# Attention in 32-wide tiles turned by VectorE, and Strassen's products in both expert layers with partial sums forked in PSUM

## The chip, the cores and the metric

The kernel runs on one core of a Trainium2 chip. Four engines compute: TensorE (PE; its weight loads are PEld), VectorE (DVE), ScalarE (ACT) and GpSimd (POOL). SyncE (SP) and POOL issue DMA transfers. Matrix products land in PSUM, eight banks of 128 partitions x 512 fp32 values; everything else lives in SBUF. The metric is the device time of one execution in microseconds.

## The reference

Inputs in fp32: q, k, v of shape (8 batches, 8 heads, 576 positions, 64), w_in (512 x 2048), w_out (2048 x 512).

```
scores = q @ k.T / 8;  kept only where 0 <= row - column < 64
attn   = softmax(scores) @ v                      # per batch and head
x      = attn, heads side by side                 # 4608 tokens x 512
h      = x @ w_in;  g = h * sigmoid(h)            # 4608 x 2048
out    = g @ w_out                                # 4608 x 512, fp32
```

## The kernel before

All products take bf16 operands. **Attention** goes by batch (8), by pairs of heads (4 a batch) and by groups of three blocks of 64 rows (3 a batch). A block of 64 query rows sees the 64 keys of its own block and of the block before, so its scores are a 128 x 64 product per head. `scores` (L359) does both heads of a pair in one matmul of 128 columns: k of the pair lies in `kt` with the two heads' 64 dimensions one above the other on the 128 partitions, and q lies in `qbd` as a block-diagonal, with zeros where the other head's dimensions are. `expo` (L377) takes the exponential on ACT, `masking` (L380) multiplies by the window's mask on DVE, `values` (L385) multiplies by v of both heads and a column of ones, `inverse` (L391) and the norm functions (L397, L414, L420) divide by the sum.

The dimensions of q and k must stand on partitions, tokens come in on partitions. Batches 0 and 1 of k and 0 to 3 of q are turned by TensorE (`turn_heads` L309, `turn_twos` L318) and copied out of PSUM (`lift_*`, L324 to L337); later ones are turned by DMA from SP (`turn_rows`, L270), q then spread by DVE (L278). The attention output is turned back by TensorE (`back`, `back_both`, L430, L441) or, from the end of batch 2 on, by DMA (`turn_o`, L435). The result, x with its 512 dimensions on partitions, is `bridge`.

**The expert layers** go by tiles of 512 tokens, nine of them. `first_layer` (L450) is plain: 16 x 4 matmuls of 512 columns a tile, `silu` (L456) after each four. `second_layer` (L459) is plain for tiles 0 to 4: 64 matmuls of 512 columns. Tiles 5 to 8 (`FAST`) use Strassen's seven products of half-size matrices in the Winograd form instead: `weight_sum` (L469) and `token_sum` (L476) make the sums of quarters on DVE, `product` (L484) makes seven times 16 matmuls of 256 columns, `keep_part` (L487) copies partial sums to SBUF and `join` (L494, L496) adds them on the way out.

**Order.** The class `Plan` places every operation on an engine's own list at build time, with costs and ranks written in the code; the chip then runs each engine's list in order, waiting on semaphores. Four PSUM banks (`at`) are for attention, four (`mp`) for the expert layers, until the attention is over. Until the first expert matmul, filler matmuls (L824) keep TensorE at work. POOL issues the loads of q, k, v and the weights, which change fp32 to bf16 on the way; SP issues two first loads, the turning DMAs and the stores.

Of the kernel before, what the change touches and what calls it, by code (L numbers as in the profile page):

```python
# [13 lines left out]

class Plan:

    def __init__(self, pools, rank, rank0, ahead):
        self.rank, self.rank0, self.pools = rank, {**rank0, **{c + "0": r for c, r in ahead.items()}}, pools
        self.queues = {}
        self.banks = [[] for _ in range(8)]
        self.count = 0
        self.now = 0.0

    def add(self, cls, us, fn, deps=(), lat=0.08, gate=None, dma=None, pool=None, table=None, b=0):
        if b > 1 and cls in ("cast", "lift", "spread", "mask", "norm"):
            lat = 0.2  # L30
        op = dict(us=us, first=self.rank[cls] + b if b or cls not in self.rank0 else self.rank0[cls], fn=fn, deps=[d for d in deps if d is not None], lat=lat, gate=gate, dma=dma,
                  pool=pool, table=table, seen=None, n=self.count, until=[], bank=None)
        self.count += 1
        self.queues.setdefault(cls, []).append(op)
        return op

    def add_filler(self, n, cls, us, fn, *args, **kw):

        for _ in range(n):
            op = self.add(cls, us, None, *args, **kw)  # L40
            op["until"], op["fn"] = [op], lambda e, op=op: fn(op)
        self.count -= n

    def done(self, ops):
        return all(d["seen"] is not None and d["seen"] <= self.now for d in ops)

    def run(self):
        head = {c: 0 for c in self.queues}
        engines = sorted({e for q in self.queues.values() for op in q for e in op["us"]})
        free = {e: 0.0 for e in engines}  # L50
        can = {e: [c for c, q in self.queues.items() if any(e in op["us"] for op in q)] for e in engines}
        table, left = "exp", self.count
        pipe = {True: 0.0, False: 0.0}
        events, order = [0.0], []
        while left:
            if not events:
                raise RuntimeError([(c, head[c], q[head[c]]["n"]) for c, q in self.queues.items() if head[c] < len(q)])
            now = self.now = heapq.heappop(events)
            while events and events[0] == now:
                heapq.heappop(events)  # L60
# [51 lines left out]
def kernel(ctx, tc, q, k, v, w_in, w_out, out):  # L112
    nc = tc.nc
# [768 lines left out]
```

## Time and profile before

| | us |
|---|---|
| median of 3 runs (lowest, highest) | 318.58 (318.53, 320.08) |
| span of the profiled execution | 315.5 |
| TensorE busy | 303.1 (96%) |
| VectorE busy | 200.5 (64%) |
| ScalarE busy | 188.4 (60%) |
| first expert matmul / last Strassen product's join, from the span's start | 23.23 / 310.61 |
| the one long gap on TensorE, in the slice from | 181 to 189 |

The profiled execution's own time is given as its span, from the first to the last instruction; the times of the runs are device times, which take in a little around it. Engine times in a group of instructions are the union of their intervals, and one instruction's duration holds its latency: matmuls are pipelined, so 16 of them in a row take far less than 16 durations. Where a price per matmul is wanted, the distance between rows of the chain or the timeline gives it.

### The profile page before, as it was taken

The numbers are of one execution on the slowest core, as the hardware profiler recorded it, in microseconds if no ns is written. First come the engines' busy times: TensorE is split into PE (matmuls) and PEld (weight loads), VectorE is DVE, ScalarE is ACT, GpSimd is POOL, SyncE is SP. The second block draws the span as 40 slices with busy tenths as digits, with TensorE's granted clock in tenths as the row PEclk, the third lists the DMA queues.
The fourth block names the chain that finished last, engine by engine and source line by source line (L and its number), as shares of the span: only waits on it lengthen the run. The fifth ranks groups of instructions, "written<-read, shape, count | busy, mean of one in ns | idle before, by whom it ended". The sixth has DMA issues, their size and how long they took to land.

```text
span 315.5 us, 6452 instructions
## 1 busy us (share of the span) xinstructions
PE 303.1 (96%) x2366; PEld 185.7 (59%) x2383; DVE 200.5 (64%) x573; ACT 188.4 (60%) x370; POOL 118.8 (38%) x159
## 2 busy tenths in 40 slices
PE   8999999999999999999999949999999999999993
PEld 4678656545565555645654535447964874684583
DVE  4684838946898899894894147956887323332422
ACT  8798786888757661767527732478346416515620
POOL 8957859676806797873465000000000000000000
PEclk9999999999999999999999988999999999999998
DMA  9999999999999999999999983310133012003003
GB/s 141 177 197 186 191 196 145 118 245 137 176 152 171 146 124 172 176 186 142 156 160 206 157 80 84 92 26 0 27 139 47 1 58 77 2 0 135 0 17 118
DMA packets 138112, 37.55 MB, mean 119 GB/s; under 512 B 122465, under 2 KB 133729, under 8 KB 138081
## 3 DMA queue, kind: packets, MB, share of 16 engines
q0 software_dynamic: 95712, 18.06, 78.1%
q1 hardware_dynamic: 42368, 19.08, 33.4%
q8 instruction: 19, 0.31, 0.4%
q14 instruction: 13, 0.10, 0.1%
HBM read 36.70 MB, written 9.44 MB: 146 GB/s over the span
## 4 chain that ended last, share of the span: by engine, by line
PE 87%; DVE 4%; DMA 4%; issue 1%; ACT 1%; POOL 0%; POOLq 0%; DVEq 0%
PE mp L450 30%; PE mp L459 20%; PE mp L484 10%; PE at L385 5%; PE at L484 5%; PE at L359 5%; PE at L450 4%; DMA vv<-in_v_dram 4%; DVE qbd L324 2%; PE at L824 1%; PE mp L824 1%; PE at L318 1%; DVE vv L345 1%; ACT qbd L324 1%; PE at L441 1%
## 5 line engine op out<-in xcount | busy, mean ns | idle before, releaser
L450 PE MATMUL mp<-bridge,w_in_sb 128*128 128x512 bf16 (+2 forms) x576 | 118.9, 355 | 0.6 <-ACT g L456 0.5
L450 PEld LDWEIGHTS <-w_in_sb 128*128 128x128 bf16 x640 | 60.1, 98 | 58.6 <-issue 1.3
L456 ACT ACTIVATE g<-mp 128x512 bf16<-128x512 f32 (+2 forms) x144 | 76.9, 552 | 26.4 <-PE mp L450 25.6
L459 PE MATMUL mp<-w_out_sb,g 128*128 128x512 bf16 x303 | 83.5, 382 | 0.6
L377 ACT ACTIVATE e<-at 128x384 bf16<-128x384 f32 x90 | 38.7, 498 | 14.1 <-PE at L359 13.5
L414 DVE TENSOR_TENSOR ox<-at,rc 64x192 bf16<-64x192 f32 x128 | 45.2, 353 | 2.4
L264 POOL DMA_DIRECT2D late<-in_k_dram x48 | 35.6, 746 | 22.6 <-DMA late<-in_k_dram 11.0
L282 POOL DMA_DIRECT2D vv<-in_v_dram x32 | 32.8, 1030 | 18.3 <-PE at L359 7.7
L459 PEld LDWEIGHTS <-g 128*128 128x128 bf16 x320 | 28.4, 98 | 17.2
L385 PEld LDWEIGHTS <-e 128*128 128x128 bf16 x288 | 22.6, 97 | 19.6 <-DVE e L380 6.7
L380 DVE TENSOR_TENSOR e<-e,mask 128x384 bf16<-128x384 bf16 x84 | 26.6, 348 | 11.8 <-ACT e L377 11.1
L385 PE MATMUL at<-vv,e 128*128 128x130 bf16 x273 | 29.8, 220 | 4.2 <-DVE e L380 4.0
L476 DVE TENSOR_TENSOR late<-g 128x512 bf16<-128x512 bf16 x32 | 13.5, 422 | 28.1 <-ACT g L456 28.0
L484 PEld LDWEIGHTS <-late 128*128 128x128 bf16 x256 | 24.8, 98 | 2.9
L264 POOL DMA_DIRECT2D late<-in_q_dram x32 | 23.8, 748 | 4.8 <-DMA vv<-in_v_dram 3.0
L359 PE MATMUL at<-qbd,kt 128*128 128x128 bf16 x252 | 24.4, 223 | 0.1
L391 DVE RECIPROCAL rc<-at 128x6 f32<-128x6 f32 x91 | 17.4, 194 | 10.6 <-PE at L385 7.5
L359 PEld LDWEIGHTS <-kt 128*128 128x128 bf16 x252 | 18.8, 100 | 8.8 <-issue 1.9
L499 ACT COPY ot<-mp 128x512 f32<-128x512 f32 x12 | 6.9, 586 | 25.9 <-PE mp L459 20.2
L484 PEld LDWEIGHTS <-g 128*128 128x128 bf16 x192 | 18.5, 98 | 2.6
L324 DVE COPY qbd<-at 64x288 bf16<-64x288 bf16 x26 | 12.5, 480 | 10.6 <-ACT qbd L324 7.1
L456 ACT ACTIVATE g<-at 128x512 bf16<-128x512 f32 x16 | 9.6, 597 | 11.6 <-PE at L450 11.6
(94 smaller groups left out, 318.8 us busy)
## 6 DMA issues: line engine op xcount, KB each, us to landing
out_dram<-ot SPq DMA_DIRECT2D x34, 256.0 KB, 2.6
vv<-in_v_dram POOLq DMA_DIRECT2D x32, 144.0 KB, 7.2
late<-in_k_dram POOLq DMA_DIRECT2D x48, 72.0 KB, 7.1
late<-in_q_dram POOLq DMA_DIRECT2D x32, 72.0 KB, 7.1
early<-in_q_dram POOLq DMA_DIRECT2D x15, 144.0 KB, 6.4
w_in_sb<-in_moe_w_in_dram POOLq DMA_DIRECT2D x8, 256.0 KB, 8.2
w_out_sb<-in_moe_w_out_dram POOLq DMA_DIRECT2D x8, 256.0 KB, 7.8
early<-in_k_dram POOLq DMA_DIRECT2D x7, 144.0 KB, 5.2
```

What stands on the lines that cost most here:

```text
L264: nc.gpsimd.dma_start(out=rows(i)[:, pj % 2, :, 64 * hh:64 * hh + 64], in_=(q, k)[kk][b, 2 * pj + hh].rearrange("(m p) d -> p m d", p=NR),)
L282: queue[e].dma_start(out=vv[b % NK][:, 2 * g0 + 1:2 * g1 + 1:2, 0:D], in_=v[b].rearrange("h s d -> (h s) d").rearrange("(g p) d -> p g d", ...
L324: copies[e](out=qbd[b % NK][64 * hh:64 * hh + 64, pj, hh].rearrange("x (p m) -> x p m", m=NM)[:, :, r::2], in_=at_bf16(op)[64 * r:64 * r + ...
L359: nc.tensor.matmul(at_sp(op)[:, x], lhsT=kt[b % NK][:, pj * S + t * 64:pj * S + t * 64 + 128], rhs=qbd[b % NK][:, pj, :, t * 64:t * 64 + 6 ...
L377: nc.scalar.activation(out=es[n % NE], in_=at_sp(op), func=ACTF.Exp, scale=scale)
L380: nc.vector.tensor_mul(es[n % NE], es[n % NE], mask0 if g == 0 else mask)
L385: nc.tensor.matmul(at_pv(op)[:, x], lhsT=es[n % NE][:, x].rearrange("p h i -> p (h i)"), rhs=vv[b % NK][:, s:s + NB + 1:NB, 0:D + 1], star ...
L414: nc.vector.tensor_mul(ox(n)[:, :, r], pv[r, :, hh, 0:D], rc[r, :, hh:hh + 1].to_broadcast([64, 3, 64]))
L450: nc.tensor.matmul(banks[bank["bank"]][:, lo:hi], lhsT=w_in_sb[:, c, ft * 128:(ft + 1) * 128], rhs=bridge[:, j * TB % NBR + lo // 64:j * T ...
L456: nc.scalar.activation(out=gts[gt][:, lo:hi], in_=banks[bank["bank"]][:, lo:hi], func=ACTF.Silu)
L459: nc.tensor.matmul(banks[bank["bank"]][:, 0:hi - lo], lhsT=gts[gt][:, m * 128:(m + 1) * 128], rhs=w_out_sb[:, f, lo:hi], start=(f == 0), s ...
L484: nc.tensor.matmul(banks[bank["bank"]][:, lo:lo + 256], lhsT=lhs, rhs=rhs, start=first, stop=last, skip_group_check=chained)
```

## The change

The kernel is written anew around the same computation.

*Layout and turning.* Four heads, 32 partitions each, make a half (`a`, two a batch). A bf16 pair of neighbouring dimensions is one 32-bit word; a 32 x 32 turn of words by VectorE puts the 32 words of 64 dimensions on 32 partitions and leaves the pair (`par`) in the free direction. So q and k are turned by `turn_third` and `turn_blocks` straight from SBUF to SBUF, and the attention output by `turn_out` into `xts`. The rows of w_in are loaded in the permuted order that this gives. TensorE and DMA turn nothing any more.

*Scores and values.* `scores` issues, for each block, half and `par`, four matmuls of 32 rows, one for each head, in four row groups, into four banks, 64 columns each. `values` issues, for each block, half of the block and half of the heads, four matmuls with 32 columns of weights, in four column groups, into one bank, 65 columns each. There are 1152 matmuls of each kind. `visit` strings eight blocks (a tile's tokens) together: scores, exponentials and masks for each `a`, values and norm in parts of three blocks, two turns.

*Expert layers.* Tile 0 is plain in both layers and tile 1 in the first. All other layers, 7 first and 8 second, use the seven products. A first layer is cut into four units (`u`) of two pairs of 128 rows each; a second layer is one unit. In a unit the first product's bank is copied by ScalarE to a second bank (`fork`), and both go on accumulating there: the second product in the copy, the sixth and fifth in the original, with the seventh, kept in SBUF, added between by VectorE (`join`), once into a third bank that then takes the fourth product. All eight banks are shared by attention and expert layers; `Unit` reserves enough for a unit that has begun.

*Loads.* The loads of batch 0 come by SP in fp32 and are cast by ACT and DVE; all others by POOL. The planner is rewritten with a priority for each operation.

```diff
+    def turn_blocks(b, a, kk, i):
+        src = nats[b % 2][a][kk][:, 384 * i:384 * i + 384].bitcast(FP32).rearrange("x (n t w) -> x n t w", n=3, t=2)
...
+            nc.vector.transpose(out=dst.rearrange("x (t n p) -> x n t p", t=2, n=3), in_=src)
...
-    def scores(op, b, pj, g):
-        for x in range(3):
-            t = 3 * g + x
-            nc.tensor.matmul(
-                at_sp(op)[:, x], lhsT=kt[b % NK][:, pj * S + t * 64:pj * S + t * 64 + 128],
-                rhs=qbd[b % NK][:, pj, :, t * 64:t * 64 + 64], start=(x == 0), stop=(x == 2),
-            )
+    def scores(bank, a, blocks):
+        for x, nb in enumerate(blocks):
+            n, s = nb % 18, (nb % 18) * 64
+            for par in range(2):
+                for h in range(4):
+                    r = slice(32 * h, 32 * h + 32)
+                    nc.tensor.matmul(
+                        banks[bank[h].idx][:, 64 * x:64 * x + 64].rearrange("k (t p) -> k t p", t=2),
+                        lhsT=kT[a][r, s:s + 128, par],
+                        rhs=qT[a][r, n // 3, :, 32 * (n % 3):32 * (n % 3) + 32, par],
+                        start=(x == 0 and par == 0), stop=(par == 1), skip_group_check=True)
...
+    def values(bank, a, blocks, x0):
+        for x, nb in enumerate(blocks):
+            b, t = divmod(nb, NB)
+            for half in range(2):
+                for h in range(4):
+                    c = (2 * x + half) * (D + 2)
+                    nc.tensor.matmul(
+                        banks[bank.idx][32 * h:32 * h + 32, c:c + D + 1],
+                        lhsT=es[a][:, h, 64 * (x0 + x) + 32 * half:64 * (x0 + x) + 32 * half + 32],
+                        rhs=vv[b % 2][:, 4 * a + h, t, 0:D + 1],
+                        start=(x == 0 and half == 0), stop=True, skip_group_check=True)
...
+    def turn_out(a, z, nb, n):
+        src = osb[a][:, 0:n].rearrange("k n d t -> k n (d t)").bitcast(FP32)[:, :, 32 * z:32 * z + 32]
+        j, s = nb // 8, nb % 8 * 64
+        nc.vector.transpose(out=xts[j % NXT][:, 2 * a + z, s:s + 64 * n].bitcast(FP32), in_=src)
...
+        for i in range(2):
+            for z in range(2):
+                nc.tensor.matmul(banks[bank.idx][:, 256 * i:256 * i + 256], lhsT=lhs(z, i), rhs=rhs(z),
+                                 start=(start and i == 0 and z == 0), stop=(z == 1), skip_group_check=True)
...
+    def fork(e, dst, src):
+        copies[e](out=dst, in_=src)
+
+    def join(dst, bank, part):
+        nc.vector.tensor_add(out=dst, in0=bank, in1=part)
...
+            m1 = prod(1, a, True, [], 0, [a])
+            m7 = prod(7, c, True, [], 0.1, [c])
+            cb = p.add({"ACT": act(512)}, lambda e, a=a, bf=bf: fork(e, at(bf), at(a)), [m1], base - 50, take=[bf], tag="fork")
+            cs = p.add({"ACT": act(512)}, lambda e, c=c, s=s: fork(e, keeps[s], at(c)), [m7] + keep_free.get(s, []), base - 50, give=[c], tag="keep")
+            m6 = prod(6, a, False, [m1, cb], 0.2)
+            m2 = prod(2, bf, False, [cb], 0.3)
+            dj = p.add({"DVE": dve(512)}, lambda _, d=d, a=a, s=s: join(at(d), at(a), keeps[s]), [m6, cs], base - 1000, take=[d], tag="join")
+            m5 = prod(5, a, False, [dj], 0.4)
+            m4 = prod(4, d, False, [dj], 0.5)
+            fj = p.add({"DVE": dve(512)}, lambda _, a=a, s=s: join(fins[s], at(a), keeps[s]), [m5] + fin_free.get(s, []), base - 1000, tag="join")
+            m3 = prod(3, a, False, [fj], 0.6)
```

In the new kernel the products of the first layer are at L438 (plain: L388), of the second at L450 (plain: L402), scores at L339, values at L361, the exponential at L346, masks at L353, norms at L371 and L374, turns of q and k at L298 to L311, of the output at L380, forks, kept copies and plain copies out at L454, joins at L457, silu at L460 (plain: L399), token sums at L407 and L411, fillers at L802.

More of the change, by code (lines that the diff above doesn't have):

```diff
@@ L12 @@
 ALU = mybir.AluOpType
-class Plan:
[L21 to L25, printed above, removed]
-        self.now = 0.0
[L28 to L34, printed above, removed]
-        return op
[L37 to L45, printed above, removed]
@@ L47, in run @@
     def run(self):
-        head = {c: 0 for c in self.queues}
-        engines = sorted({e for q in self.queues.values() for op in q for e in op["us"]})
+        engines = ["PE", "ACT", "DVE", "POOL", "SP"]
         free = {e: 0.0 for e in engines}
-        can = {e: [c for c, q in self.queues.items() if any(e in op["us"] for op in q)] for e in engines}
-        table, left = "exp", self.count
-        pipe = {True: 0.0, False: 0.0}
+        ready = {e: [] for e in engines}
+        table, pipe = "exp", 0.0
@@ L835 @@
[L835 to L850 removed]
+    w_in_sb = keep.tile([128, 4, d_ff], BF16, name="w_in_sb")
```

1263 lines of the change are left out of this document (615 added, 648 removed).

## The prediction

> **What bounds the kernel now.** I read the page first (busy shares and slices), then the table of stretches, the chain that ended last, the groups of instructions by form, and the timelines of TensorE, ScalarE and VectorE for prices.
>
> ```profile
> span 315.5 us, 6452 instructions
> PE 303.1 (96%) x2366; PEld 185.7 (59%) x2383; DVE 200.5 (64%) x573; ACT 188.4 (60%) x370; POOL 118.8 (38%) x159
> ...
> PE   8999999999999999999999949999999999999993
> ```
>
> TensorE is busy in every slice but one (the stall near 185 us). The median of the runs, 318.58 us, is 3.1 over this span; I take these 3.1 as what lies around any span and add them at the end. Differences under 0.5% (1.6 us) I count as no change.
>
> The table of stretches (length; busy time and count of PE, PEld, DVE, ACT, POOL; clock; DMA share; GB/s) has the start, a plain tile in the middle, and a Strassen tile late, where the attention is over:
>
> ```profile
> 0.00:23.20 23.20, 21.34 (x267) 13.93 (x268) 15.30 (x53) 19.98 (x39) 18.93 (x32) 1.00 1.38 171
> 98.70:131.60 32.90, 32.74 (x220) 17.70 (x221) 29.77 (x87) 18.41 (x33) 27.10 (x35) 1.00 2.15 158
> 258.50:284.50 26.00, 26.00 (x177) 17.23 (x176) 9.08 (x22) 11.78 (x22) 0.00 (x0) 1.00 0.11 41
> ```
>
> A tile with attention costs 32.9 us, one without 26.0. TensorE is full in both, so the time is the sum of its columns plus whatever it waits for. Prices of columns, from the chain that ended last (start, length, what):
>
> ```profile
> 259.36 3.45 PE mp L450 x16
> ...
> 302.71 4.37 PE at L484 x40
> ...
> 310.61 0.42 DVE ot L496
> ```
>
> A 512-column matmul takes 3.45/16 = 0.2156 us, a 256-column Strassen one 4.37/40 = 0.109 us, so halving the width costs nothing. The last product ends at 310.6; 4.9 us of join and store follow.
>
> **The change, part by part.**
>
> *Dense matmuls.* Before: first layer 9 tiles x 64 x 0.2156 = 124.2, plain second layer 5 x 64 x 0.2156 = 69.0, Strassen second layer 4 x 112 x 0.109 = 48.8; 242.0 us. After: plain first layer for tiles 0 and 1 in narrower pieces of the same columns (28.0), plain second layer for tile 0 (13.8), Strassen in 7 first layers and 8 second layers, 15 x 112 x 0.109 = 183.1; 224.9 us. All of it lies on TensorE's path. Gain 17.1.
>
> *Attention on TensorE.* Removed: about 700 matmuls of 64 to 130 columns and the turns by identity. From the first expert matmul at 23.23 to 310.6 there are 287.4 us, of which 242.0 are dense: 45.4 went to attention and stalls. Added: 1152 score products (32 rows, 64 columns, four row groups side by side) and 1152 value products (four column groups of 32): 576 quads of four. No such quad stands in the trace. The nearest are the transposes of L430, 64-column matmuls in two column groups, against L441, the same width on the whole array (TensorE's timeline: start, length with the last one's latency, count; then the two groups by form, whose second number is the mean ns of one):
>
> ```profile
> 3.89 1.49 PE L824 MATMUL at<-ident 128*128 128x384 bf16 x4
> 5.17 1.49 PE L824 MATMUL mp<-ident 128*128 128x384 bf16 x4
> ...
> 7.25 0.81 PE L824 MATMUL mp<-ident 128*128 128x384 bf16 x4
> 7.89 0.81 PE L824 MATMUL at<-ident 128*128 128x384 bf16 x4
> ...
> 17.96 0.28 PE L430 MATMUL at<-ident,ox 128*64 128x64 bf16 x6 [0.50 <-DVE ox L420]
> 18.18 0.34 PE L366 MATMUL mp<-bias,ident 128*128 128x384 bf16 x1
> ...
> 23.23 0.82 PE L450 MATMUL mp<-bridge,w_in_sb 128*128 128x192 bf16 x8
> ...
> 47.54 0.25 PE L441 MATMUL at<-twoi,ob 128*128 128x64 bf16 x3
> ```
> ```profile
> L441 PE MATMUL at<-twoi,ob 128*128 128x64 bf16 x60 | 4.9, 194 | 0.1
> ...
> L430 PE MATMUL at<-ident,ox 128*64 128x64 bf16 x54 | 2.6, 203 | 0.5 <-DVE ox L420 0.5
> ```
>
> L441: (0.25 - 0.194)/2 = 28 ns a matmul, one after the other. L430: (0.28 - 0.203)/5 = 16 ns, so two groups do run side by side. A quad is therefore bounded by 32 ns (four as fast as two now, two pairs in the time of one) and 4 x 28 = 112 ns (none overlaps). I take 4 x 16 = 64 ns, the rate that tiled matmuls have shown: 30 quads before the first expert matmul, 546 behind it, 546 x 0.064 = 34.9 us.
>
> A change of tiling costs too: the six of L430 need 6 x 16 = 0.1 us, yet the next matmul starts 0.22 behind the first. I take 0.1 us for each change (bounds 0 and 0.2). The order of the built program has 49 runs of scores or values between other matmuls; about 90 changes lie behind the first expert matmul: 9.0 us (0 to 18). Attention and its changes, 43.9, are thus no cheaper than before's 45.4 with its stalls in it.
>
> The Trainium skill, "TensorE: Matmul & The Clock Gate", section on the 56 ns gap, says that start-to-start never drops below about 25 ns however small the matmul. By it a quad is an estimated 100 ns and the sum below would be 327; the 16 ns of L430 disagree.
>
> *Start.* Fillers keep TensorE running as before; the built program has 54 of 512 columns and 30 quads in five runs ahead of the first expert matmul. The rows of L824 show 0.32 us for 384 columns early (four in 1.28, the distance of their rows) and 0.16 from 7.25 on, so 0.43 and 0.2156 for 512: 12 cold ones until 6.6 us, 42 x 0.2156 = 9.1, 30 x 0.064 = 1.9, five runs x 0.2 = 1.0: 18.6 us instead of 23.23. It holds if the first 1.3 MB of q, k and v and the first half of the input weights are there; the DMA rate says so:
>
> ```profile
> GB/s 193 196 196 193 197 196 196 197 197 195 196 196 196 193 197 201 195 225 183 189 198 198 198 191 169 184 177 185 195 187 174 165 181 194 194 234 168 155 175 159
> ```
>
> (16 to 32 us, bytes as they land.) At 190 GB/s, 2.4 MB take 12.6 us. All of batch 0 and both layers' weights must land by about 40 us (3.5 MB as fp32 and 2 x 2.1 MB as bf16, 7.7 MB, 40 us at this rate): just on time. I allow 2 us of waiting there, bounds 0 and 10. The DMA queues get lighter: 20 transposes of q and k and 16 of the output leave SP, and q and k come in rows of 512 bytes instead of 256. POOL issues 163 loads instead of 142:
>
> ```profile
> L264 POOL DMA_DIRECT2D late<-in_k_dram x48 | 35.6, 746 | 22.6 <-DMA late<-in_k_dram 11.0 <-DMA vv<-in_v_dram 6.5 <-DMA w_out_sb<-in_moe_w_out_dram 2.8
> ```
>
> At 0.75 us a batch of 21 takes 16 us on POOL, half of the 9/8 tile for which it is needed, so I cost the queue at nothing; each load waits for the turns or values of the batch two before, a full batch earlier.
>
> *ScalarE and VectorE in a steady tile.* Prices by form, and two back-to-back runs from the timelines:
>
> ```profile
> L456 ACT ACTIVATE g<-mp 128x512 bf16<-128x512 f32 x112 | 65.7, 597 | 25.9 <-PE mp L450 25.4
> ...
> L380 DVE TENSOR_TENSOR e<-e,mask 128x384 bf16<-128x384 bf16 x84 | 26.6, 348 | 11.8 <-ACT e L377 11.1
> ...
> L476 DVE TENSOR_TENSOR late<-g 128x512 bf16<-128x512 bf16 x32 | 13.5, 422 | 28.1 <-ACT g L456 28.0
> ...
> L391 DVE RECIPROCAL rc<-at 128x6 f32<-128x6 f32 x91 | 17.4, 194 | 10.6 <-PE at L385 7.5 <-ACT e L377 0.5 <-PE at L359 0.4
> ...
> L377 ACT ACT_TABLE_LOAD x6 | 7.7, 1283 | 0.9 <-DVE ox L414 0.8
> ...
> L499 ACT COPY ot<-mp 128x512 f32<-128x512 f32 x12 | 6.9, 586 | 25.9 <-PE mp L459 20.2 <-issue 3.6 <-DMA raw<-late 2.0
> ...
> L347 DVE COPY vv<-vv 64x2304 bf16<-64x2304 bf16 x6 | 5.3, 884 | 4.7 <-DMA vv<-in_v_dram 4.5
> ...
> L496 DVE TENSOR_TENSOR ot<-mp,late 128x512 f32<-128x512 f32 x4 | 2.8, 692 | 6.6 <-ACT late L487 6.5
> ...
> L420 DVE TENSOR_TENSOR ox<-mp,rc 128x384 bf16<-128x384 f32 x3 | 1.6, 541 | 0.0
> ```
> ```profile
> 217.95 2.79 ACT L377 ACTIVATE e<-at 128x384 bf16<-128x384 f32 x7
> ```
> ```profile
> 219.07 0.89 DVE L380 TENSOR_TENSOR e<-e,mask 128x384 bf16<-128x384 bf16 x3
> ```
>
> Seven exponentials of 384 take 2.79 us, 0.38 each behind the first; with 128 columns more, about 0.49. ScalarE per tile: 16 silus, 8 exponentials, 10 forks and kept copies, 2 outputs, 36 x 0.49, and two table loads of 1.28: 20.2 us. VectorE per tile at means: 10 joins x 0.69, 16 token sums and 4 input sums x 0.42, 4 masks of 1024 (0.35 + 640 columns at 0.58 ns, the step from L380 to L476: 0.72), 6 norms x 0.5 with 6 reciprocals x 0.2, 2 shifts of v x 0.8 (L347's 0.88 for 2304 columns, 2048 here), 10.7 turns of q and k and 4 of the output. The trace shows no turn by VectorE: from below 192 words cost no less than a 192-column bf16 mask would, 0.24; from above twice L420's price for 384, 1.1. I take 0.3 and 0.4, L420's rate of about 1.2 ns a column over some 0.07. Sum 28.8 us by means, nearer 24 back to back (three masks take 0.89, not 1.05).
>
> TensorE per tile: 224 x 0.109 = 24.4, 64 quads 4.1, eight changes 0.8: 29.3. So TensorE stays the bound, VectorE close behind it. What is late next is latency: in a Strassen unit the first product is forked by ScalarE (0.59) before the sixth can add to it, and two joins (0.69 each) precede the fifth and third. The built order starts two units together, then has nothing else: first join after two forks, a silu table load, a silu and a kept copy, 2 x 0.49 + 1.28 + 2 x 0.49 + 0.69, some 4 us and hand-overs, against nine products x 0.44 = 3.9; about 0.5 us open. At the other end the last values of a visit are followed by a reciprocal, a norm and two turns (0.2 + 0.4 + 2 x 0.4) with 0 to 20 products of 0.109 to cover them: 1 us on average. So 1.5 us a tile (bounds 0.5 and 4), 7 tiles: 10.5.
>
> *End.* The last join, copy and store: 4.9 as before.
>
> *Sum.* 18.6 + 224.9 + 34.9 + 9.0 + 2.0 + 10.5 + 4.9 = 304.8; with 3.1 around it 307.9.
>
> **Rivals.**
>
> 1. *Quads cheap*: four groups run as four, 32 ns. L430's pair speaks for overlap, nothing shows four. 546 x 0.032 = 17.5 less: 290.
> 2. *VectorE bounds the tile* (chain and engine both): if a turn takes twice what I took, VectorE needs 28.8 + 10.7 x 0.3 + 4 x 0.4 = 33.6 us a tile against TensorE's 29.3 + 1.5 = 30.8; 7 x 2.8 = 19.6 more: 327. For it: 29.77 of 32.9 us busy in the stretch above without stalling TensorE; against: back-to-back prices are lower.
> 3. *Slower, one mechanism*: row-grouped loads of 128 columns do not overlap, a quad costs 112 ns, 546 x 0.048 = 26.2 more: 334. It decides from 64 + 10.7/0.546 = 84 ns on. For it: no row shows row groups; against: column groups do overlap. The skill's floor of 25 ns (the page named above) would have the same effect.
> 4. *Strassen gives nothing*, because the narrow matmuls cost more: excluded by 0.109 against 0.2156/2.
>
> **How the numbers follow.** Forecast 0.46 (300 to 316), rival 1 0.18 (286 to 300), rival 2 0.19 (316 to 332), rival 3 0.13 (318 to 336), anything else 0.04, slow. The time is the forecast's 308. The range 292 to 327 leaves out the ends of rivals 1 and 3, some 0.2; the forecast's own is 300 to 316. Faster (under 317): 0.46 + 0.18 + a tenth of rival 2, 0.66. Same: 0.07, from the low ends of rivals 2 and 3. Slower: 0.27.
>
> **What would show it.** First expert matmul near 18.6 us; Strassen products at 0.109; runs of 64 score products lasting about 1.0 us beside their latency; tile to tile 31 us in the middle; VectorE under 29 us a tile; gaps of 0.5 us at the first join and 1 us behind the last values. Wrong if a turn takes over 0.6 us, a quad over 84 ns, or the tile is over 33 us because TensorE waits for joins or silus.

## The result: 7% slower

The changed kernel takes 341.17 us (median of 4 runs, 340.07 to 342.4) beside 318.89 us for the kernel before: a ratio of 1.070, interval 1.066 to 1.074. The prediction was 308, with a range of 292 to 327. The profiled execution took 341.61 us, 1.7 over its span.

The page of the changed kernel: totals, slices of TensorE and of its granted clock, and the chain that ended last, by engine.

```profile
span 339.9 us, 10402 instructions
PE 289.0 (85%) x4416; PEld 226.8 (67%) x4422; DVE 233.8 (69%) x603; ACT 208.8 (61%) x386; POOL 110.7 (33%) x170
...
PE   8374217999979679996999999999979989999994
...
PEclk9967556999999989998999999999999999999998
...
PE 46%; DVE 23%; SPq 11%; ACT 8%; DMA 5%; issue 4%; POOL 1%; DVEq 0%; ACTq 0%
```

Before, TensorE was full from the second slice on but for one stall; now slices 2 to 7 (8 to 60 us) are one to seven tenths busy, and the granted clock falls to half there. SP's queue, which carries only the loads of batch 0 and the stores, is 11% of the chain. The table of stretches (length; busy time and count of PE, PEld, DVE, ACT, POOL; clock; DMA share; GB/s), over the start and two steady tiles:

```profile
10.00:25.00 15.00, 8.08 (x93) 3.54 (x95) 4.09 (x11) 5.49 (x14) 4.00 (x6) 0.77 0.99 152
25.00:41.00 16.00, 6.49 (x103) 4.15 (x103) 4.87 (x15) 5.27 (x11) 4.58 (x6) 0.66 0.88 135
41.00:53.00 12.00, 2.96 (x64) 2.18 (x64) 6.20 (x20) 3.73 (x12) 3.51 (x5) 0.50 1.06 182
```
```profile
220.70:251.80 31.10, 29.14 (x481) 23.91 (x481) 26.65 (x67) 21.52 (x39) 3.32 (x4) 1.00 0.38 67
251.80:282.20 30.40, 28.75 (x480) 23.78 (x480) 23.45 (x54) 21.33 (x39) 0.00 (x0) 1.00 0.25 46
```

In these stretches of the start no engine is busy for over 55% of the time; in the steady tiles TensorE is busy for 94 to 95%, at 30.4 to 31.1 us each. What the start waits for stands in SP's timeline (start, length, queue, line, transfer), and below that, the landing of one of its last pieces in the chain that ended last:

```profile
2.75 0.85 SPq L265 DMA_DIRECT2D gsum<-in_q_dram  x1
3.64 8.77 SPq L279 DMA_DIRECT2D wsum<-in_v_dram  x2
12.45 5.10 SPq L265 DMA_DIRECT2D wsum<-in_k_dram  x1
...
22.26 4.24 SPq L279 DMA_DIRECT2D wsum<-in_v_dram  x1
26.54 7.13 SPq L265 DMA_DIRECT2D wsum<-in_k_dram  x1
...
41.18 3.79 SPq L276 DMA_DIRECT2D gsum<-in_v_dram  x1
```
```profile
38.98 13.79 DMA wsum<-in_v_dram
```

The seventeen loads of batch 0, 3.5 MB in all, are still being issued at 41 us, and one of v's last pieces lands at 52.8. TensorE's timeline has the first expert matmul, the bulk of tile 0's first layer, and the first product of tile 2:

```profile
32.51 1.48 PE L388 MATMUL bank<-xt,w_in_sb 128*128 128x192 bf16 x8
...
60.44 9.03 PE L388 MATMUL bank<-xt,w_in_sb 128*128 128x192 bf16 x128
...
125.41 1.73 PE L438 MATMUL bank<-xt,w_in_sb 128*128 128x256 bf16 x8 [0.74 <-DVE o L374]
```

The start of the last of these, which my sum puts at 18.6 + 54.0 (dense work of tiles 0 and 1) + 10.4 + 2.7 (162 quads and 27 changes) + 2.0 = 87.7 us, came at 125.4. From there to the end of the span it takes 214.5 us, 217.1 in my sum. So the whole miss lies in front of tile 2: +37.7 there, -2.6 behind it, and -1.4 around the span.

### The profile page after: what moved, and what is told of

It is laid out like the page before. It is cut to its first block, busy times and chain, and to the rows that moved or that the text cites. A ratio compares the mean times of both kernels' runs of the same rounds, so it can differ in the third digit from the quotient of the medians.

```text
span 339.9 us, 10402 instructions
## 1 busy us (share of the span) xinstructions
PE 289.0 (85%) x4416; PEld 226.8 (67%) x4422; DVE 233.8 (69%) x603; ACT 208.8 (61%) x386; POOL 110.7 (33%) x170
## 4 chain that ended last, share of the span: by engine, by line
PE 46%; DVE 23%; SPq 11%; ACT 8%; DMA 5%; issue 4%; POOL 1%; DVEq 0%; ACTq 0%
PE bank L438 22%; PE bank L450 15%; SPq L265 7%; DVE o L374 5%; PE bank L388 5%; DMA wsum<-in_v_dram 4%; SPq L279 4%; DVE es L353 3%; PE bank L402 3%; DVE gsum L407 3%; DVE xt L380 2%; ACT es L346 2%; ACT L346 2%; PE bank L339 2%; DVE kT L308 1%
## 5 line engine op out<-in xcount | busy, mean ns | idle before, releaser
L450 PEld LDWEIGHTS <-gsum 128*128 128x128 bf16 x512 | 47.6, 98 | 11.1 <-DVE gsum L407 3.5
L460 ACT ACTIVATE g<-bank 128x512 bf16<-128x512 f32 x84 | 48.7, 617 | 4.6 <-PE bank L438 3.6
L438 PEld LDWEIGHTS <-wsum 128*128 128x128 bf16 x448 | 44.5, 99 | 10.5 <-issue 2.6
L450 PE MATMUL bank<-wsum,gsum 128*128 128x256 bf16 x384 | 47.3, 273 | 2.8 <-DVE gsum L407 2.0
L438 PE MATMUL bank<-xsum,wsum 128*128 128x256 bf16 x336 | 46.5, 279 | 1.2 <-DVE xsum L411 1.0
L279 POOL DMA_DIRECT2D vv<-in_v_dram x28 | 25.5, 930 | 58.6 <-PE bank L361 50.0
L346 ACT ACTIVATE es<-bank 128x512 bf16<-128x512 f32 (+3 forms) x96 | 39.5, 496 | 6.0 <-PE bank L339 5.9
L438 PEld LDWEIGHTS <-w_in_sb 128*128 128x128 bf16 x336 | 32.9, 99 | 13.8 <-issue 7.1
L450 PEld LDWEIGHTS <-g 128*128 128x128 bf16 x384 | 36.6, 98 | 7.2 <-issue 2.3
L454 ACT COPY ot<-bank 128x512 f32<-128x512 f32 x23 | 13.4, 591 | 44.2 <-PE bank L450 29.8
L438 PE MATMUL bank<-xt,w_in_sb 128*128 128x256 bf16 x224 | 32.7, 281 | 6.5 <-DVE xt L380 3.6
L457 DVE TENSOR_TENSOR bank<-bank,part 128x512 f32<-128x512 f32 x36 | 24.5, 695 | 19.9 <-ACT part L454 10.3
L450 PE MATMUL bank<-w_out_sb,g 128*128 128x256 bf16 x256 | 33.9, 273 | 2.2 <-ACT bank L454 2.1
L407 DVE TENSOR_TENSOR gsum<-g 128x512 bf16<-128x512 bf16 x64 | 26.9, 421 | 11.2 <-ACT g L460 7.1
L388 PE MATMUL bank<-xt,w_in_sb 128*128 128x192 bf16 (+2 forms) x320 | 33.3, 266 | 0.6 <-ACT es L346 0.6
L353 DVE TENSOR_TENSOR es<-es,strip 128x1024 bf16<-128x1024 bf16 (+3 forms) x48 | 25.4, 546 | 11.5 <-ACT es L346 10.8
L339 PE MATMUL bank<-qT,kT 32*128 32x64 bf16 x1152 | 14.3, 194 | 21.8 <-DVE qT L301 17.4
L388 PEld LDWEIGHTS <-w_in_sb 128*128 128x128 bf16 x320 | 28.5, 103 | 4.1 <-issue 1.5
L454 ACT COPY part<-bank 128x512 f32<-128x512 f32 x36 | 20.7, 594 | 16.4 <-PE bank L450 16.3
L374 DVE TENSOR_TENSOR o<-bank,rc 128x384 bf16<-128x384 f32 (+2 forms) x56 | 29.4, 527 | 1.9
```

Of the source, the lines that this page charges most:

```text
L279: queue[e].dma_start(out=dst, in_=v[b, :, 128 * g:128 * g + 128].rearrange("h p d -> p h d"))
L346: nc.scalar.activation(out=es[a][:, h, 0:64 * n], in_=banks[bank.idx][:, 0:64 * n], func=ACTF.Exp, scale=scale)
L353: nc.vector.tensor_mul(t, t, strip[:, s:s + n].rearrange("k n i -> k (n i)").unsqueeze(1).to_broadcast([128, 2, 64 * n]))
L374: nc.vector.tensor_mul(osb[a][:, x0:x0 + n].rearrange("k n d t -> k n t d"), at_values(bank, n)[:, :, :, 0:D], rcs[w][:, 0:n].unsqueeze(3) ...
L388: nc.tensor.matmul(banks[bank.idx][:, i * n:i * n + n], lhsT=w_in_sb[:, c, 128 * ft:128 * ft + 128], rhs=xts[j % NXT][:, c, lo:hi], start= ...
L407: (nc.vector.tensor_sub if i else nc.vector.tensor_add)(out=dst[i], in0=a, in1=b)
```

## Experiments

Each time is that of one execution, except where an interval is given; beside it stands the kernel before, timed together with it. The kernel before alone ran from 316.1 to 320.2 us in 13 executions, so single times that differ by 1% say little. "Tile 2" is the start of its first layer's first product on TensorE's timeline. A "third" is a load of 192 rows of q or k of four heads (`load_third`); a "filler" is a matmul that only keeps TensorE at work.

| kernel | us | before | tile 2 at |
|---|---|---|---|
| the change | 341.17 | 318.89 | 125.4 |
| e1: v by POOL | 330.65 | 317.38 | 113.3 |
| e2: all of batch 0 by POOL | 318.88 | 317.38 | 102.2 |
| e3: weights moved behind batch 1 | 356.05 | 317.38 | 141.1 |
| e4: q and k ahead of v | 340.70 | 317.38 | 125.4 |
| e5: loads as they were | 348.12 | 318.67 | 132.1 |
| e6: e2, weights early | 320.48 | 318.67 | 104.4 |
| e7: e6, first thirds by SP | 323.69 | 318.67 | 107.8 |
| e9: e2, first layers plain | 341.52 | 318.67 | |
| e10: POOL held until SP is done | 338.33 | 316.37 | 121.1 |
| e11: e2, weights by rows | 314.68, ratio 0.992 (0.989 to 0.994) | 317.93 | 96.6 |
| e12: e11, q and k by head | 322.02 | 316.37 | 105.1 |
| e13: the change, both forms | 322.24 | 317.45 | 105.8 |
| e14: e12, fewer fillers | 318.80, ratio 1.004 (1.000 to 1.007) | 317.45 | 100.3 |
| e15: the change, weights' form alone | 355.62 | 317.45 | 139.4 |
| e16: e14, loads in order of need | 315.29, ratio 0.990 (0.985 to 0.995) | 317.93 | 100.0 |

In all of these but e9, tile 2 to the end of the span takes 213.0 to 215.5 us (214.5 in the changed kernel). The start alone makes their differences.

### Which queue, and which pieces

Two theories stand in the expectations: A, that SP's queue is slow by itself, and B, that it competes with POOL's queue for the sixteen transfer engines. e1 and e2 take batch 0 off SP's queue, v alone or all of it; POOL loads it with the cast in the transfer, straight into `vv` and `nats`, among the pieces of the first layer's weights:

```diff
-    load_first_v(0)
-    load_first_v(1)
...
+        load_pairs(0, {0: (0, 1), 2: (2,), 4: (3, 4)}[pi0])
...
```


> Batch 0's v goes through the software queue with the cast in the transfer, straight into its place in vv, five issues of POOL among the first pieces of the first layer's weights; q and k stay on SP's hardware queue with the cast on the engines. Theory A (SP's queue is held by the 256-byte pieces of v: each of them, and the q or k third behind it, holds SP for 4 to 9 us): SP issues its twelve thirds at 0.7 to 2 us each and is done by about 15 us; the first expert matmul comes at 19 to 23 us instead of 32.5, its bulk before 40 instead of 60, and the time is 308 to 322. Theory B (the two queues share 16 transfer engines, and the weights take what batch 0 lacks): the bytes are the same, the last third lands at 40 us or later, the bulk of the first expert layer begins at 55 or later, and the time is 335 to 345.

```diff
-    load_first(0)
...
+        load_rows(0, (pi0 // 2,), -50)
...
```


> All of batch 0 (q, k and v) goes through the software queue with the cast in the transfer, straight to where the turns and the value products read it; SP loads nothing, no cast runs on ACT or DVE, and POOL issues 17 transfers more among the 12 of the first layer's weights. Theory A (SP's queue is what held the start): the first expert matmul at 20 to 26 us (before's was at 23.2 with the same kind of loads), the bulk of the first layer before 45, the time 306 to 322. Theory B (transfer capacity): the written bytes fall from 7.7 to 6.0 MB up to the second layer's weights, a fifth, so the bulk comes at 48 to 55 instead of 60 and the time is 328 to 336.

e1 fell between: without any v on SP, its twelve thirds still took until 25.5 us to issue. e2 gave back 21 to 22 us. So SP's loads, with the casts that go with them, are what held the start, and v's small pieces are not the whole of it.

e4 puts the five pieces of v last on SP:

```diff
-    load_first_v(0)
-    load_first_v(1)
     load_first(1)
-    load_first_v(2)
     load_first(2)
-    load_first_v(3)
-    load_first_v(4)
+    for g in range(5):
+        load_first_v(g)
```

> The order on SP alone is changed: the twelve thirds of q and k first, the five pieces of v behind them. Theory A (the pieces of v hold the queue): the thirds are issued at 0.7 to 2 us each and are done by 15 us, v takes the next 25 to 30 us, so the value products and with them the first expert matmul are no earlier than 30 us; the time is 335 to 348, about the same as the changed kernel. Theory B (competition with the weights): the thirds too take 2 to 5 us each while the weights are in flight, the last of them lands at 25 us or later, v at 45 to 55; the time is the same 335 to 348.

No gain; both theories had said so, and the thirds behind the first four again took 1.5 to 5.8 us each.

e3 and e5 were to hold the software queue until SP was done, by a dependence given to the planner (e3 for the first layer's weights alone):

```diff
-        return p.add({"POOL": us}, fn, deps, n_soft[0], dma=dma, tag=tag, after=after)
+        return p.add({"POOL": us}, fn, list(deps) + firsts[-1:], n_soft[0], dma=dma, tag=tag, after=after)
```


> The software queue's weights wait until the last third of q and k of batch 0 has landed, so that SP's hardware queue has the 16 transfer engines to itself; the loads and their order on SP are those of the changed kernel. Theory A (SP's queue is slow by its own pieces): SP still takes 40 us or more to issue its 17 loads, its issues of v still take 4 to 9 us each, the weights then land some 30 us after that, and the time is 355 to 375. Theory B (competition): alone on the engines the 3.5 MB land by 14 to 20 us, the weights begin there, the first expert matmul comes at 24 to 30, and the time is 320 to 340.

> The loads of batch 0 are those of the changed kernel, in its order on SP, and every transfer of the software queue (weights, batch 1 and all later ones) waits until the last of them has landed: SP's queue has the 16 transfer engines to itself. Theory A (the 256-byte pieces of v, or the queue's own pace, hold SP): the 17 issues still take 35 us or more, v's 4 to 9 us each. Theory B (the two queues share the transfer engines, and each third gets through only between the software queue's packets): the 3.5 MB are issued by 12 to 16 us and landed by 14 to 20 us, as the plan of the prediction has it, and the visits of tile 0 are done by 28. The time is no test here, since the weights start 15 us or more later: 335 to 350 by theory B, 360 or more by A.

Neither held anything. The planner's dependences order each engine's list; the chip waits only where data are shared, and nothing here was. e3 moved batch 1 and the second layer's weights ahead of the first layer's; e5 has the changed kernel's loads, with SP's issues at the same moments within 0.8 us, and 81 fillers instead of 54. Its 348 us are 7 more than the changed kernel took; I put them down to the rest of the start's order, which was not tried further. Neither run tells the theories apart. e10 makes POOL read a word of the last piece:

```diff
+    holds.append(p.add({"POOL": 0.2}, lambda _: nc.gpsimd.tensor_copy(out=held[64:128], in_=stage_v8[:, 0, 0:4]), firsts[-1:], -50, tag="hold"))
```


> The loads of the changed kernel in their order, but POOL first copies four words of the last piece of v that SP loads, so that none of its own transfers is issued before that piece has landed. (In the two runs before that were to hold the software queue, only the order of its transfers changed, since nothing in the program made POOL wait.) Theory A (SP's queue is slow by itself: the 256-byte pieces of v, or eight transfers in flight that each take long): SP's 17 issues still take 35 us or more. Theory B (competition with the software queue): they take 12 to 18 us, the last lands by 14 to 20 us, a third takes under 2 us from issue to cast once it is its turn. Under B the weights then start at about 18 us and the time is 325 to 345; under A at 45 or later and the time is 350 to 375.

```profile
33.26 0.19 POOL L797 COPY held<-gsum 64x4 f32<-64x4 f32 x1 [31.67 <-DMA gsum<-in_v_dram]
```

The last load landed at 33 us, and the last issue ended at 27.5: neither theory's number. With nothing of POOL's in flight SP needs over 30 us, not 12 to 18, so competition adds some 20 us to a queue that is slow by itself. The stretches of e10 show what slows it:

```profile
14.00:16.00 2.00, 2.00 (x6) 0.76 (x5) 1.17 (x4) 1.62 (x4) 0.00 (x0) 0.50 0.26 95
...
24.00:26.00 2.00, 1.35 (x19) 0.60 (x7) 0.83 (x4) 1.07 (x2) 0.00 (x0) 1.00 0.72 190
26.00:28.00 2.00, 1.16 (x7) 0.39 (x7) 1.47 (x5) 0.37 (x1) 0.00 (x0) 1.00 0.27 98
```

In the first and third of these nearly all packets are those of the thirds, in the second v's 256-byte ones are in flight too. The small pieces are the fast ones. The thirds, with packets of 1536 bytes, keep the sixteen transfer engines at 0.26 to 0.27 of their time: the work of four. The kernel before loads q and k by SP at 2 to 4 us too, in packets of the same 1536 bytes, as 96 partitions:

```profile
2.00:4.00 2.00, 2.00 (x8) 0.99 (x7) 1.89 (x7) 1.97 (x3) 1.95 (x4) 1.00 0.98 264
```

Share 0.98, 264 GB/s, nearly all of it from SP's queue (363 of 365 packets). The packets themselves are as fast in both: the trace gives a median of 65 ns for one of 1536 bytes. But in e10 four of them are in flight at once for most of the first and third stretch, in the kernel before about sixteen. What differs is the form. A third (`load_third`, L263) reads `(q, k)[kk][b, 4 * a:4 * a + 4, 192 * i:192 * i + 192].rearrange("h (p c) d -> h p (c d)", c=6)`, an outermost loop of four heads; each piece of the first layer's weights (`load_w_in`, L281) has four runs of 32 rows.

### The form of the transfers

The Trainium skill, "DMA: Bandwidth & Descriptors", section "Why a DMA increments its semaphore by 16 and not by 1", states it: the number of engines is the largest up to 16 that divides the slowest dimension on both sides. By this rule a third runs on four engines; 0.26 to 0.27 of sixteen engines' time, 4.2 to 4.3 of them, agrees.

e11 changes the weights' pieces on e2, e12 batch 0's q and k as well, each to 32 partitions as the outermost loop:

```diff
-        rows = w_in[256 * a:256 * a + 256].rearrange("(h z d) f -> z h d f", h=4, z=2)[z]
-        queue[e].dma_start(out=w_in_sb[:, c, lo:hi], in_=rows[:, :, lo:hi])
+        rows = w_in[256 * a + 64 * h:256 * a + 64 * h + 64].rearrange("(z d) f -> d z f", z=2)
+        queue[e].dma_start(out=w_in_sb[32 * h:32 * h + 32, 2 * a:2 * a + 2, lo:hi], in_=rows[:, :, lo:hi])
```


> As the kernel with all of batch 0 in the software queue, but the first layer's weights come as 16 transfers of 32 partitions (one run of 64 rows of w_in each, as two groups of 32) instead of 12 of 128 partitions (four runs of 32 rows). Theory D (the transfers whose 128 partitions are made of four runs of 32, the thirds and these weights, each leave 350 to 400 packets of 4 bytes and hold their queue): the 4-byte packets up to 38 us fall from 11,289 to about 6,000, the last weights land at 30 to 33 us instead of 37, and the time is 312 to 316. If the packets of 4 bytes cost nothing, or come from something else, the last weights land at 35 to 39 and the time is 317 to 321, the same.

```diff
+            out=nats[b % 2][a][kk][32 * h:32 * h + 32].rearrange("p (i x) -> p i x", i=3),
+            in_=(q, k)[kk][b, 4 * a + h].rearrange("(i p c) d -> p i (c d)", i=3, c=6))
```


> As the kernel before it, with batch 0's q and k too in transfers of 32 partitions: 16 transfers of one head (1152 words to a partition in three runs) instead of 12 thirds of four heads, all ahead of v and the weights. Theory D: the 4-byte packets up to 38 us fall under 2,000, the queue writes 170 to 190 GB/s as in the kernel before the change instead of 140, all of w_in is there by 27 to 30 us, and the time is 306 to 312, under the kernel before the change. If D is wrong, all of q and k stands ahead of the first visit and the first expert matmul is later, 24 to 28 us, the weights land at 36 to 40, and the time is 318 to 325.

e11 took 314.93 us at first (the table has its repeat), within the 312 to 316 expected. Its theory D blames packets of 4 bytes: up to 38 us the trace has 11,289 of them in e2, 6,782 in the repeat of e11 and 2,247 in e12, so on POOL's queue these runs do not part them from the number of engines. On SP's queue they are no rival: e10's thirds are slow with only four of them in a stretch of 2 us. e12 missed: its time is the one written for a wrong D. From 5 to 11 us its queue moved 131 GB/s, not 170 to 190. q and k were turned at 14.4 us, but the fillers that stand ahead of the first scores kept TensorE until 22.8, and the first 32 expert matmuls then ran at half rate. The decisive run, e13, keeps the changed kernel's two queues, staging and casts, and changes both forms as in these two diffs (into `stage_qk` for batch 0). It changes three smaller things with them: batch 0's q and k stand ahead of v on SP, which alone gave nothing (e4); batch 1's come by head as well; and the planner sets the first scores behind the placing of v.

> The changed kernel with its two queues, its casts and its staging as they were, but with the form of the transfers changed whose outermost loop has four turns: q and k of batches 0 and 1 come by head (32 partitions, three runs each, 16 transfers a batch) instead of by third of four heads, and the first layer's weights by 64 rows (32 partitions) instead of by four runs of 32. Held alone, the thirds kept the transfer engines at a busy share of 0.27 (95 GB/s), while v's pieces reached 0.72 (190 GB/s). Theory E (a transfer is dealt out over the engines by its outermost loop, so one with four turns uses four of the sixteen): q and k of batch 0 have landed by 16 us and v by 26 even beside the weights, the first expert matmul comes at 20 to 26 us and the time is 306 to 320. If what slows SP is the sharing of engines with the software queue and not the form, q and k land at 25 us or later, v at 45 or later, and the time stays at 330 to 342.

```profile
3.00:10.00 7.00, 7.00 (x30) 3.01 (x29) 1.86 (x5) 2.21 (x3) 4.23 (x8) 1.00 0.97 206
10.00:20.00 10.00, 5.09 (x46) 2.34 (x46) 2.81 (x8) 1.85 (x4) 5.44 (x10) 0.93 1.12 257
```

206 and 257 GB/s where the changed kernel moved 135 to 152 from 10 to 41 us; SP's last load was issued at 26 us instead of 41. The time fell to 322.24: of the 22 us lost, 17.5 to 19 came back, and tile 2 began 19.6 us earlier. That is just over the number expected, and the first expert matmul was later than expected, 35.5 us instead of 20 to 26. The second half's first scores waited 9.5 us for their q, until 24.6, and the first values came only at 30.5:

```profile
24.60 0.51 PE L345 MATMUL bank<-qT,kT 32*128 32x64 bf16 x24 [9.45 <-DVE qT L307]
30.53 0.24 PE L367 MATMUL bank<-vv,es 128*32 128x65 bf16 x2 [5.42 <-DVE es L359]
...
35.50 1.46 PE L394 MATMUL bank<-xt,w_in_sb 128*128 128x192 bf16 x8
```

No run changed the form of q and k alone.

e15 makes the weights' edit alone in the changed kernel, and my expectation was wrong by 20 us and in sign (slower, not faster):

> The changed kernel with only the first layer's weights in the form of 64 rows and 32 partitions, and 54 fillers; the thirds of batch 0 stay on SP as they were. Theory E: the weights leave the four engines that the thirds use much earlier (16 transfers at some 200 GB/s, done by 14 to 18 us), so SP's issues get nearer to what they took alone: the last at 25 to 35 us instead of 41, the last landing by 32 to 42 instead of 53, and the time is 322 to 335. If the form of the weights does not matter for SP, its last issue is at 40 or later again and the time is 337 to 345.

It is the slowest but one, 355.62. With all sixteen engines kept busy by the weights, the thirds on their four got less, not more: SP's two issues of v, behind the first four thirds, took 15.85 us (8.77 in the changed kernel), and the trace's packets give the thirds 28 to 31 GB/s from 8 to 20 us, against 26 to 64 in the changed kernel from 8 to 18 and 95 alone.

```profile
3.58 15.85 SPq L279 DMA_DIRECT2D wsum<-in_v_dram  x2
```
So in this one run the narrow transfers lost more beside wide ones than beside narrow ones. From 16 us on POOL also loads batch 1's thirds, narrow themselves, and later the second layer's weights, all of it earlier than in the changed kernel; how much of the delay that is was not parted.

### What else the start holds

e6 moves the weights of e2 ahead of the second thirds; e7 is e6 with the first thirds by SP.

```diff
     load_rows(0, (0,), -50)
     load_pairs(0, (0, 1))
+    for pi0, pi1 in ((0, 2), (2, 4), (4, 8)):
+        for c in range(4):
+            ld = soft(SOFT, lambda e, c=c, pi0=pi0, pi1=pi1: load_w_in(e, c, 256 * pi0, 256 * pi1), dma=0.39 * (pi1 - pi0))
...
     load_rows(0, (1,), -50)
```

> As the kernel with all of batch 0 in the software queue, with the twelve pieces of the first layer's weights moved ahead of batch 0's second and third thirds. If the start is bound by the sum of bytes at some 140 GB/s and by nothing else, the first expert layer of tile 0 has work for its first 192 tokens as soon as the weights are there (by 28 us instead of 37), and TensorE is busy from there: its second layer begins 3 to 6 us earlier than 49.7, tile 2 begins at 96 to 99 instead of 102.2, and the time is 312 to 316. If instead the later thirds become the last thing waited for, tile 2 begins at 102 to 106 and the time is 318 to 323.

> As the kernel with the weights early, but the four first thirds of q and k come over SP's queue with casts on the engines (the first four issues of the changed kernel), all else over the software queue. Theory B (competition): the four thirds land one after the other at about 4 us each once the weights are in flight, as in the changed kernel (casts at 5.8, 10.2, 15.0, 18.0 us), the first scores of the second four heads are as late as 18 us, and the time is that of the kernel with the weights early, within 3 us. Theory A (SP's queue is slow only behind v): the four thirds land by 7 us, the first scores come 5 us earlier than 17.4, and the time is 2 to 5 us shorter than that kernel's.

e6 gained nothing, with tile 2 at 104.4 against 102.2: the second outcome written for it. e7 took 3 us more than e6: its four thirds landed one after another beside v and the weights, with casts at 5.7, 9.0, 13.8 and 16.5 us.

e14 is e12 with batch 1 by head too and `range(50)` instead of `range(90)` for the fillers; e16 has all transfers in the order in which they are needed and takes tile 0's first layer 256 tokens at a time:

```diff
+    load_whole(0, -50)
+    load_pairs(0, range(5))
...
-    plain_first(0, [(0, 192), (192, 384), (384, 512)], [1, 1, 2])
+    plain_first(0, [(0, 256), (256, 512)], [1, 1])
```

> As the kernel with heads and row weights in the software queue, with batch 1 by head too and 50 filler matmuls ahead of the first scores instead of 59 (90 at most before). In that kernel q and k were turned at 14.5 us and the first v's placed at 18, but the fillers, which stand ahead of the first scores on TensorE, ended only at 22.8 us, and the clock then fell to half. If the fillers are what held it: first scores at 17 to 19 us, the first expert matmul at 21 to 24, the bulk of the first layer of tile 0 from 28 to 32 instead of 40.5, and the time is 308 to 313, below the kernel before the change by 1 to 3 per cent. If the wait is for v and the weights instead, the bulk begins at 36 or later and the time is 317 to 322.

> As the last kernel in the software queue (heads, row weights), with the transfers in the order in which they are needed: all of q and k of batch 0, all of v, both layers' weights, then batch 1; the visits of tile 0 stand ahead of its expert layers on TensorE, the first layer takes pairs in the order in which their weights come, 256 tokens at a time, and fillers stand between the visits too. At the 200 GB/s that transfers of this form reached, q, k and v (1.77 MB) are there by 14 to 17 us after a start at 3, the first layer's weights by 27 to 30, the second's by 38 to 42. If the landing of bytes is what bounds the start: the first layer of tile 0 runs from 22 to 27 us to 38 to 42 (45.6 in the kernel with thirds and row weights), tile 2 begins at 90 to 94 instead of 97.8, and the time is 308 to 312, 1.5 to 3 per cent below the kernel before the change. If batch 1, now last, becomes the wait, tile 1's attention holds TensorE after the second layer of tile 0, tile 2 begins at 96 to 101, and the time is 315 to 319.

> The kernel with all of batch 0 in the software queue by thirds and the first layer's weights by rows, timed in rounds: its one time was 314.93 beside 316.37 for the kernel before the change. If that was no chance, its ratio is 0.992 to 0.998 with the tile period of 30.5 us that all these kernels share from tile 2 on; if it was, 0.998 to 1.005.

e14 brought the first scores to 14.3 us and took about 3 us less than e12, less of a gain than expected: the first layer's bulk began at 35.0 us, not at 28 to 32, and visits of attention stood between the layers of tile 0. e16 ran the first layer of tile 0 without a break (below) and ended the second at 58.0 us instead of 62.6 in the repeat of e11. But batch 1, now last, landed near 54, TensorE waited several times for its scores and values, up to 1.2 us each, and tile 2 began at 100: the second outcome by its numbers.

```profile
29.08 14.15 PE L393 MATMUL bank<-xt,w_in_sb 128*128 128x256 bf16 x128
```
e11 and e16 are about 1% below the kernel before and below the changed kernel too. That is clear of their intervals, but little.

### What the seven products are worth

e9 undoes one part of the change in e2, the Strassen first layers of tiles 2 to 8:

```diff
-            fast_first(j)
+            plain_first(j, [(0, 256), (256, 512)], [1, 1])
```


> As the kernel with all of batch 0 in the software queue, with the first expert layer of tiles 2 to 8 plain: eight products of each pair instead of seven, no forks, joins or sums of token halves in that layer; the second layer keeps its seven. If TensorE's columns set the period, each of the seven tiles takes 16 x 0.109 = 1.74 us more, less what the joins made TensorE wait (some 0.8 us a tile in the steady tiles): the period goes from about 30.5 to 31.4 to 32.3 us and the time from 318.9 to 325 to 331. If the chain of forks and joins eats what the seven products save, the time stays at 317 to 321 or falls below.

22.6 us more (21.3 if each is set against the kernel before that was timed with it), 3.0 to 3.2 us a tile, where columns explain 1.74. Three stretches of e9: the gap in front of a plain first layer, and the layer in two parts:

```profile
205.00:207.70 2.70, 0.56 (x24) 0.32 (x14) 2.56 (x9) 0.68 (x1) 2.59 (x4) 0.86 0.80 212
207.70:216.00 8.30, 8.28 (x49) 6.04 (x49) 1.94 (x4) 2.99 (x6) 0.74 (x1) 0.63 0.79 52
216.00:224.40 8.40, 8.40 (x80) 7.52 (x78) 1.67 (x5) 5.96 (x10) 0.00 (x0) 1.00 0.01 2
```

TensorE waits 2.2 us for the turned attention output, the clock is then granted at 0.63, and 49 products take the time of 80. In e2 the stretch of a Strassen first layer (196 to 208 us) has a clock of 1.00. So the part was worth more than its columns: without it a gap opens in front of the layer, and the clock falls. Such a gap of 1.1 to 2.2 us stands in front of all seven plain layers, and the clock was at half for 3.4 to 6.8 us at five of them; the last two gaps cost no clock. In e2 the one gap of this kind, 2.5 us in front of tile 3, was followed by half the clock for 3.4 us too. An estimate from the mean clocks, 0.950 of e9's 339.8 us and 0.972 of e2's 317.2, gives 8 us lost to the clock, and 7 x 1.74 = 12.2 to columns: 20 of the 21 to 23. Why the gap opens was not tried.

## Why the prediction was wrong

**The step that failed is the start: "All of batch 0 and both layers' weights must land by about 40 us ... just on time. I allow 2 us of waiting there, bounds 0 and 10", and with it "At 190 GB/s, 2.4 MB take 12.6 us".** The 190 GB/s came from the kernel before, whose transfers had another form; I carried a rate over to transfers whose form I had not looked at. The changed kernel moved 135 to 152 GB/s from 10 to 41 us, batch 0's loads landed at 53 us, and every stage up to tile 2 was late by 14 to 38 us. e2 shows the loads as the cause; e10 shows their form at work, and e13, with both forms changed, takes 19.6 of the 37.7 us away. No rival had it; all four were about TensorE and VectorE. What e11 and e16 still lose against 87.7, 9 to 12 us, I take to be partly the landing of 6 MB at up to 200 GB/s and partly order; it was not parted, and stays open. A smaller slip had no effect that the runs show: POOL's 163 loads replace 150 in the trace of the kernel before, not 142.

**Dense matmuls: right.** Strassen products take 0.109 us, plain ones 0.2156, as before.

**Quads: mis-sized; rival 1 had the price.** Two runs of 64 scores and one of 64 values from TensorE's timeline, then groups by form (the second number behind the bar is the mean ns of one):

```profile
237.07 0.71 PE L339 MATMUL bank<-qT,kT 32*128 32x64 bf16 x64
237.72 0.61 PE L450 MATMUL bank<-wsum,gsum 128*128 128x256 bf16 x4
...
240.88 0.72 PE L339 MATMUL bank<-qT,kT 32*128 32x64 bf16 x64
...
242.07 0.72 PE L361 MATMUL bank<-vv,es 128*32 128x65 bf16 x64
242.72 0.61 PE L450 MATMUL bank<-wsum,gsum 128*128 128x256 bf16 x4
```
```profile
L339 PE MATMUL bank<-qT,kT 32*128 32x64 bf16 x1152 | 14.3, 194 | 21.8 <-DVE qT L301 17.4 <-DVE rc L371 4.3
L308 DVE STREAM_TRANSPOSE kT<-nat 128x192 f32<-128x192 f32 x36 | 12.4, 356 | 0.7 <-PE bank L339 0.6
L311 DVE STREAM_TRANSPOSE qT<-nat 128x192 f32<-128x192 f32 x36 | 11.9, 342 | 0.0
L380 DVE STREAM_TRANSPOSE xt<-o 128x256 f32<-128x256 f32 x28 | 10.5, 420 | 0.3
```

(0.71 - 0.194)/63 = 8.2 ns a score matmul, 33 a quad, not 64; the 64 values take 0.01 us more. Both changes of tiling are in the 0.65 us from 237.07 to 237.72; a tile's attention takes 4 x 0.65 = 2.6 us where I had 4.9 (4.1 for the quads and 0.8 for the changes). Rival 3, and with it the floor of 25 ns that the prediction cites from the Trainium skill, "TensorE: Matmul & The Clock Gate", is refuted for matmuls in four row or column groups.

**Stalls a tile: low, inside the bounds.** 214.5 - 7 x 24.4 dense - 6 x 2.6 attention - 4.9 at the end leaves 23.2 us of waits, 3.3 a tile, not 1.5. Cheap quads and dear waits nearly cancel. So the period, 29.5 to 31.0 us from the second of these tiles on (32.7 for the first) where I had 31, was right by luck, with two terms wrong in opposite ways.

**VectorE: right.** The rows above have turns of 192 words at 342 to 356 ns and of 256 words at 420 (I took 0.3 and 0.4), and its busy time is 23 to 27 us a tile; rival 2 falls.

**Rival 4** stays excluded: by e9 the seven products of the first layers are worth 3 us a tile.

## What to carry to other kernels

A rate of bytes belongs to a form of transfer: look at the outermost loop of every new transfer, and at the share of the transfer engines that one of the same form kept busy, before taking a rate from another kernel's row. When a rewrite moves the start as well as the steady part, sum them apart and ask of each load when it lands; a steady tile that is right to 2% is no help against 38 us in front of it. An undo of one part can cost more than the part's own work: in e9 it opened gaps on TensorE, and the clock was lower at five of the seven.

## What was not expected of the hardware

- Transfers of 128 partitions in four runs of 32 reached 95 to 99 GB/s alone (share 0.26 to 0.27), and 28 to 31 beside transfers that used all engines; a stretch with v's 256-byte pieces in flight, whose outermost loop has 64 or 128 turns, reached 190.
- In e9 a wait of 2.2 us on TensorE was followed by 8.3 us at a granted clock of 0.63.
- Matmuls of 64 or 65 columns in four row or column groups follow each other at 8.2 to 8.3 ns.
